# Attention's transposes as pairs of 64-row products into two banks, with a new order of the instructions

## The chip, the cores and the metric

The kernel runs on one core of one Trainium2 chip. The metric is the time of one execution in microseconds (us) on the device; a kernel is run several times and the median counts. Five engines work side by side, each through its own queue in order: TensorE (PE in the profile, its loading of stationary operands PEld), VectorE (DVE), ScalarE (ACT), GpSimd (POOL) and SyncE (SP, which here issues the DMAs).

## The reference

Four batches of eight heads go through an attention whose weak scores are cut off; its output goes through two feed-forward layers.

```python
scores = scale * np.matmul(q, k.transpose(0, 1, 3, 2))      # (4, 8, 576, 576), head size 64
thresh = np.max(scores, axis=-1, keepdims=True) - tau
scores = np.where(scores >= thresh, scores, -1000000000.0)
scores = scores - np.max(scores, axis=-1, keepdims=True)
attn = np.exp(scores)
attn = attn / (np.sum(attn, axis=-1, keepdims=True) + 1e-09)
out = np.matmul(attn, v)
...
g = h * np.tanh(sp)                 # h = x @ w_in (512 to 2048), sp = softplus(h); then g @ w_out
...
return (silu * val @ w_out)         # silu and val from x @ w_gate, x @ w_val (512 to 1536)
```

All numbers are float32.

## The kernel before

The first part of the program is the attention, the second the two layers (`moes`); the change is in the attention alone. The attention works on 16 pairs of heads. The queries of a pair are cut into chunks of 64 per head: chunks 0 to 3 of 128 rows of work per head, and a last one that holds both heads' last 64 queries, so that there are nine row blocks of 128 x 576 scores, numbered 0 to 8. In this text S, R, H, E, M, T, V, A and x are the kinds of step, with the number of the block behind them:

- S0, S2, S4, S6 (`scores`, line 97) make two blocks each with 64-row products, the two heads by turns, one on the upper and one on the lower 64 rows of the array; S8 makes one block with products over all 128 rows. A block takes two neighbouring banks of the eight in PSUM, so S0 to S6 take four.
- R (`rowmax`, L105, DVE) reads a block's maximum, H (`thresh`, L109, POOL) makes the threshold, E (`expo`, L115, ACT) the exponential, M (`mask`, L123, DVE) masks it and gives the block's two banks back.
- T (`trans`, L151 and L148, PE) transposes the masked weights of a pair of blocks, 128 x 128 at a time, nine such squares for chunks 0 to 3 and four and a rest for the last; V (`evac`, L157, L160, L164, ACT) copies the squares from PSUM into the tile `pt`. T takes one bank. Squares are taken in groups of three.
- A (`av`, L174, PE) multiplies `pt` with the values: A0 for the first four blocks (256 queries), A1 for the other five (320). Each is cut in two parts (`PARTS`). It takes one bank until x copies it out (x0 on ACT, L204; x1 on DVE, L202).
- At the end of a pair POOL adds a small number to the row sums (`added`, L178), DVE takes reciprocals (`recip`, L182, L183) and turns them (L187), and DMAs spread them over the rows.

What stands when on each engine is written out by a planner (`Plan`): each step has a rank from the table `RANK`, which differs for the first, second and last pair and is one row for the rest, and the planner places banks and steps by its own table of costs. Engines then work strictly in that order. Beside the attention the planner puts steps that prepare the first weights (L498 to L512, the names cn, cu, cl) and pieces of the layers' input (xo) on DVE, ACT and POOL.

Of the kernel before, what the change touches and what calls it, by code (L numbers as in the profile page):

```python
# [16 lines left out]
P = 128  # L17
# [19 lines left out]
def attention(tc, cst, q, k, v, x, beside, parked, S=576):  # L37
# [100 lines left out]
    def trans(p, c, m0, n):  # L138
        d = st[p]
        if m0 == 0 and c in (0, 2):  # L140
            d["pt", c // 2] = pw.tile([P, 9, 320], F32, tag="pt", name=f"pt{p}_{c // 2}", bufs=SLOTS["pt"])
        g = bank(p, "T", c, m0)
        d["g", c, m0] = g.rearrange("p (m c) -> p m c", m=4)
        for m in range(n):
            o = 128 * (m0 + m)
            if c == 4 and m0 == 4:
                if m == 0:
                    nc.tensor.transpose(g[0:64, 0:128], d["pp", c][:, o:o + 64], idf)  # L148
                    continue
                o -= 192  # L150
            nc.tensor.transpose(g[:, 128 * m:128 * m + 128], d["pp", c][:, o:o + 128], idf)  # L151

    def evac(p, c, m0, n):
        d = st[p]
        t, g = d["pt", min(c // 2, 1)], d["g", c, m0]
        if c < 4:
            nc.scalar.copy(out=t[:, m0:m0 + n, 128 * (c % 2):128 * (c % 2) + 128], in_=g[:, 0:n])  # L157
        elif m0 == 0:
            for h in range(2):
                nc.scalar.copy(out=t[:, 5 * h:5 * h + 4, 256:320], in_=g[:, :, 64 * h:64 * h + 64])  # L160
        else:
            for h in range(2):
                a = slice(64 * h, 64 * h + 64)
                nc.scalar.copy(out=t[a, 4, 256:320], in_=g[a, h, a])  # L164
# [71 lines left out]
    for p in range(NP):  # L236
# [14 lines left out]
        for i in range(9):  # L251
            c, h = divmod(i, 2)
            if not h:
                n = 2 if i < 8 else 1
                t = .77 if i < 8 else .81
# [5 lines left out]
            for m0, n in (((0, 3),), ((3, 3), (6, 3)))[h] if i < 8 else ((0, 4), (4, 2)):  # L261
                g = (p, "T", c, m0, 0)
                op("PE", (.109 * n, .109 * n + .164), trans, c, m0, n, key=("T", c, m0), after=[("M", i)] + [("T", 2 * min(c // 2, 1), 0)] * (m0 > 0 or c not in (0, 2)) + [("T", c, 3)] * (m0 == 6) + [("T", 4, 0)] * (c == 4 and m0 > 0), take=["b1"] + ["pt"] * (m0 == 0 and c in (0, 2)), free=["pp"] * (m0 == (6 if c < 4 else 4)))
                op("ACT", (.367, .485) if c < 4 else (.545, .658) if m0 == 0 else (.33, .44), evac, c, m0, n, key=("V", c, m0), after=[("T", c, m0)], free=[g])
            if i in (3, 8):
                u = int(i == 8)
                ready = [("V", y, z) for y in ((0, 1), (2, 3))[u] for z in (0, 3, 6)] + [("V", 4, 0), ("V", 4, 4), ("A", 0)] * u + [("v", "load")]
# [845 lines left out]
```

## Time and profile before

| | before |
|---|---|
| median of 3 runs | 1075.63 us (1073.8 to 1077.04) |
| the profiled execution's own time | 1075.19 us |
| its span, first to last instruction | 1073.4 us |
| PE busy | 1052.0 us, 98% of the span |
| DVE, ACT, POOL busy | 775.1, 649.0, 262.6 us |
| first scores, last product of the attention | 7.05 us, about 278 us |

The span is what the profile shows of an execution; 1.8 us of the execution's own time lie around it. Busy time of PE holds the time in which products wait on one another in the array, so that a busy PE need not be a PE at its limit. The profile's lines name engine, line of the program, operation and tiles (out<-in).

### The profile page before, as it was taken

What the parts mean: (1) busy time and instruction counts of PE and PEld (TensorE: products, weight loads), DVE (VectorE), ACT (ScalarE), POOL (GpSimd) and SP (SyncE); (2) the same over time, 40 slices, a digit from 0 to 9 for tenths busy, and PEclk for the clock granted to TensorE, in tenths of its full rate; (3) what the DMA queues carried; (4) which work ended last, traced back from release to release, by engine and by line L of the source; (5) the groups of instructions that cost most, each with busy time, mean ns of one, the idle gap of its engine ahead of it and who ended that gap; (6) DMA issues with size and microseconds to landing.
All of it is one profiled execution on the core that took longest, in us unless ns stands there. A gap on an engine that the chain in (4) does not pass through costs nothing.

```text
span 1073.4 us, 17930 instructions
## 1 busy us (share of the span) xinstructions
PE 1052.0 (98%) x6532; PEld 949.0 (88%) x6532; DVE 775.1 (72%) x1436; ACT 649.0 (60%) x1286; POOL 262.6 (24%) x401
## 2 busy tenths in 40 slices
PE   7999999999999999999999999999999999999998
PEld 6666676676899999999999999999999999999997
DVE  7888888888788465557377776974778686786645
ACT  6788888888877675455346555664445454444331
POOL 3467667676211120012011001110111011010000
PEclk9999999999999999999999999999999999999999
DMA  3234222243867876577567696688888788887793
GB/s 95 86 98 145 75 84 70 80 145 108 312 260 279 286 254 217 178 256 257 175 216 254 207 344 240 247 312 303 313 287 297 258 297 311 277 296 244 234 309 122
DMA packets 56775, 236.90 MB, mean 221 GB/s; under 512 B 8816, under 2 KB 9072, under 8 KB 56688
## 3 DMA queue, kind: packets, MB, share of 16 engines
q1 hardware_dynamic: 56688, 235.77, 63.5%
q8 instruction: 51, 0.84, 0.3%
q14 instruction: 36, 0.29, 0.1%
HBM read 197.92 MB, written 37.82 MB: 220 GB/s over the span
## 4 chain that ended last, share of the span: by engine, by line
PE 91%; ACT 3%; issue 1%; DVE 1%; DVEq 0%; ACTq 0%
PE ha L808 23%; PE y L934 18%; PE hb L808 17%; PE y L936 14%; PE banks L174 7%; PE banks L97 7%; PE banks L151 5%; ACT pt L157 1%; ACT e L115 1%; PE banks L148 0%; ACT g L841 0%; DVE g L844 0%; ACT c L853 0%; DVE sm L105 0%; ACT L853 0%
## 5 line engine op out<-in xcount | busy, mean ns | idle before, releaser
L512 POOL TENSOR_TENSOR cn<-cn,cl 128x512 int32<-128x512 int32 x68 | 93.4, 1374 | 631.3 <-DVE cn L509 449.1
L934 PE MATMUL y<-g,wo 128*128 128x384 f32 x1152 | 227.8, 334 | 1.6 <-DVE wo L535 0.9
L934 PEld LDWEIGHTS y<-g,wo 128*128 128x128 f32 x1152 | 202.1, 188 | 2.3 <-DVE wo L535 1.1
L952 DVE TENSOR_TENSOR acc<-y,acc 128x512 f32<-128x512 f32 (+2 forms) x163 | 100.0, 626 | 108.2 <-PE y L936 63.5
L936 PE MATMUL y<-wo,g 128*128 128x512 f32 (+1 forms) x654 | 166.6, 391 | 0.0
L808 PE MATMUL hb<-xp,wb 128*128 128x384 f32 x720 | 138.4, 334 | 0.0
L808 PE MATMUL ha<-xp,wb 128*128 128x384 f32 x720 | 138.3, 334 | 0.0
L936 PEld LDWEIGHTS y<-wo,g 128*128 128x128 f32 x654 | 120.5, 188 | 18.9
L123 DVE SCALAR_TENSOR_TENSOR pp<-banks,sm,e 128x576 f32<-128x576 f32 x144 | 114.9, 815 | 21.2 <-ACT e L115 15.1
L808 PEld LDWEIGHTS ha<-xp,wb 128*128 128x128 f32 x720 | 126.6, 188 | 3.1
L844 DVE TENSOR_TENSOR g<-c,g 128x384 fp32r<-128x384 f32 x168 | 103.1, 615 | 36.0 <-ACT g L841 35.3
L808 PEld LDWEIGHTS hb<-xp,wb 128*128 128x128 f32 x720 | 126.4, 188 | 1.5
L841 ACT CAST g<-c 128x384 fp32r<-128x384 f32 x168 | 86.2, 514 | 63.1 <-DVE c L877 31.0
L115 ACT ACTIVATE e<-banks,sm 128x576 f32<-128x576 f32 x144 | 106.5, 754 | 12.9 <-DVE sm L105 12.2
L105 DVE TENSOR_REDUCE sm<-banks 128x1 f32<-128x576 f32 x144 | 101.7, 751 | 13.4 <-PE banks L97 13.1
L853 ACT ACTIVATE c<-c 128x384 f32<-128x384 f32 x144 | 75.4, 525 | 52.0 <-DVE c L829 51.5
L157 ACT COPY pt<-banks 128x384 f32<-128x384 f32 x192 | 89.9, 490 | 24.4 <-PE banks L151 22.6
L151 PE MATMUL banks<-idf,pp 128*128 128x128 f32 x656 | 94.8, 280 | 3.6 <-DVE pp L123 3.1
L819 ACT COPY u<-ha 128x384 f32<-128x384 f32 x60 | 28.8, 480 | 112.9 <-PE ha L808 112.8
L151 PEld LDWEIGHTS banks<-idf,pp 128*128 128x128 f32 x656 | 71.1, 141 | 25.7 <-ACT pt L157 8.3
L174 PE MATMUL banks<-pt,vn 128*64 128x256 f32 (+1 forms) x640 | 88.4, 413 | 0.9 <-ACT pt L164 0.9
L808 PE MATMUL ha<-xp,wa 128*128 128x384 f32 x360 | 73.5, 340 | 0.8 <-ACT acc L204 0.8
(90 smaller groups left out, 1576.6 us busy)
## 6 DMA issues: line engine op xcount, KB each, us to landing
raw<-in_dram SPq DMA_DIRECT2D x68, 512.0 KB
xp<-x20T SPq DMA_DIRECT2D x24, 768.0 KB
xp<-x21T SPq DMA_DIRECT2D x20, 768.0 KB
xp<-x22T SPq DMA_DIRECT2D x20, 768.0 KB
xp<-x20B SPq DMA_DIRECT2D x18, 768.0 KB
xp<-x10T SPq DMA_DIRECT2D x15, 768.0 KB
xp<-x21B SPq DMA_DIRECT2D x15, 768.0 KB
xp<-x22B SPq DMA_DIRECT2D x15, 768.0 KB
```

Of the source, the lines that this page charges most:

```text
L105: nc.vector.tensor_reduce(out=d["nm"][:, i:i + 1], in_=d["s", i], op=ALU.max, axis=AX.X, negate=True)
L115: nc.scalar.activation(out=e, in_=d["s", i], func=AF.Exp, bias=d["nm"][:, i:i + 1])
L123: nc.vector.scalar_tensor_tensor(out=d["pp", c][:, 576 * h:576 * h + 576], in0=d["s", i], scalar=d["th"][:, i:i + 1], in1=d["e", i], op0=A ...
L151: nc.tensor.transpose(g[:, 128 * m:128 * m + 128], d["pp", c][:, o:o + 128], idf)
L157: nc.scalar.copy(out=t[:, m0:m0 + n, 128 * (c % 2):128 * (c % 2) + 128], in_=g[:, 0:n])
L174: nc.tensor.matmul(out=d["av", u][64 * h:64 * h + 64, 0:n], lhsT=d["vn"][:, 5 * h + j], rhs=d["pt", u][:, 5 * h + j if j < 4 else 4, 0:n], ...
L512: nc.gpsimd.tensor_tensor(out=self.n[key], in0=self.n[key], in1=self.l[key], op=ALU.add)
L808: nc.tensor.matmul(out=tiles[bank, q], lhsT=w[:, a, w0 + P * d:w0 + P * d + P], rhs=x[:, z, d], start=k in (1, 5, 2) and d == 0 and y == 0 ...
L844: (V if GLOW[L] == "DVE" else nc.gpsimd).tensor_tensor(out=tiles["g", j, s][:, 1], in0=tiles[nm, q], in1=f(tiles["g", j, s][:, 0]), op=ALU ...
L934: nc.tensor.matmul(out=y[:, 0:C], lhsT=w[:, a, P * d:P * d + P], rhs=h[:, x], **m)
L936: nc.tensor.matmul(out=y[:, c0:c1], lhsT=h[:, x, P * d:P * d + P], rhs=w[:, a, c0:c1], **m)
L952: V.tensor_tensor(out=a, in0=y, in1=a, op=ALU.add)
```

## The change

A square of 128 x 128 is no longer transposed by one product over 128 rows but by two over 64 rows, upper and lower by turns, into two neighbouring banks; the stationary operand is 64 rows of 128 columns, the moving one a 64 x 64 identity. Groups are four and five squares in place of three, three and three, so that a chunk has two V in place of three, of 512 and 640 elements a row in place of 384. T takes two banks in place of one. `pt` has ten columns of squares in place of nine. The planner's costs of the transposes (`TCOL`), of the copies and of the turns between kinds of products are new, and `RANK` with all of its numbers. The layers' code is the same.

```diff
-            d["pt", c // 2] = pw.tile([P, 9, 320], F32, tag="pt", name=f"pt{p}_{c // 2}", bufs=SLOTS["pt"])
-        g = bank(p, "T", c, m0)
-        d["g", c, m0] = g.rearrange("p (m c) -> p m c", m=4)
+            d["pt", c // 2] = pw.tile([P, 10, 320], F32, tag="pt", name=f"pt{p}_{c // 2}", bufs=SLOTS["pt"])
+        at = 512 * plan.got[p, "T", c, m0][0]
+        g = d["g", c, m0] = bk[:, at:at + 1024].rearrange("p (b m c) -> p b m c", b=2, m=8)
         for m in range(n):
-            o = 128 * (m0 + m)
-            if c == 4 and m0 == 4:
-                if m == 0:
-                    nc.tensor.transpose(g[0:64, 0:128], d["pp", c][:, o:o + 64], idf)
-                    continue
-                o -= 192
-            nc.tensor.transpose(g[:, 128 * m:128 * m + 128], d["pp", c][:, o:o + 128], idf)
+            for b in range(2):
+                rows, o = slice(64 * b, 64 * b + 64), 128 * (m0 + m)
+                if c == 4 and m0 == 4:
+                    a, e = 512 - 64 * b, 64 + 64 * b
+                    nc.tensor.transpose(g[0:e, b, 0], d["pp", c][rows, a:576], idf[rows, rows])
+                else:
+                    nc.tensor.transpose(g[:, b, m], d["pp", c][rows, o:o + 128], idf[rows, rows])
...
         if c < 4:
-            nc.scalar.copy(out=t[:, m0:m0 + n, 128 * (c % 2):128 * (c % 2) + 128], in_=g[:, 0:n])
+            nc.scalar.copy(out=t[:, m0:m0 + n, 128 * (c % 2):128 * (c % 2) + 128].rearrange("p m (b c) -> p b m c", b=2), in_=g[:, :, 0:n])
         elif m0 == 0:
-            for h in range(2):
-                nc.scalar.copy(out=t[:, 5 * h:5 * h + 4, 256:320], in_=g[:, :, 64 * h:64 * h + 64])
+            nc.scalar.copy(out=t[:, :, 256:320].rearrange("p (h m) c -> p h m c", h=2)[:, :, 0:4], in_=g[:, :, 0:4])
...
-            for m0, n in (((0, 3),), ((3, 3), (6, 3)))[h] if i < 8 else ((0, 4), (4, 2)):
+            for m0, n in (((0, 4),), ((4, 5),))[h] if i < 8 else ((0, 4), (4, 1)):
...
-    TURN = dict(ST=.106, SA=.175, TS=.08, TA=.09, AS=.15, AT=.15)
+    TURN = dict(ST=.02, SA=.15, TS=.02, TA=.1, AS=.15, AT=.15)
...
+TCOL = .065
```

The new ranks move steps at three places that matter below. The first is PE in the middle of the attention, from S0 of a pair to its S2 (pp_2 and pp_4 hold the weights of the pair before, the L97 rows with kh and qh are scores). Before:

```order
L151 MATMUL banks<-idf,pp_2_973 128x128 [waits DVE_49]
L151 MATMUL banks<-idf,pp_2_973 128x128 x2
L151 MATMUL banks<-idf,pp_4_1048 128x128 x4
L151 MATMUL banks<-idf,pp_3_1031 128x128 [waits Activation_49]
L151 MATMUL banks<-idf,pp_3_1031 128x128 x5
L151 MATMUL banks<-idf,pp_3_1031 128x128 [waits Activation_49]
L151 MATMUL banks<-idf,pp_3_1031 128x128 x2
L97 MATMUL banks<-kh_943,qh_997 128x320 [waits Activation_49]
L97 MATMUL banks<-kh_943,qh_997 128x320 [waits DVE_49]
```

And now:

```order
L151 MATMUL banks<-idf,pp_3_1162 128x64 [waits DVE_49]
L151 MATMUL banks<-idf,pp_3_1162 128x64 x7
L151 MATMUL banks<-idf,pp_4_1183 128x64 [waits Activation_49]
L151 MATMUL banks<-idf,pp_4_1183 128x64 x7
L151 MATMUL banks<-idf,pp_3_1162 128x64 [waits Activation_49]
L151 MATMUL banks<-idf,pp_3_1162 128x64 x9
L97 MATMUL banks<-kh_1053,qh_1034 128x320 [waits Activation_49]
L97 MATMUL banks<-kh_1053,qh_1034 128x320 [waits DVE_49]
```

Sixteen squares stood there, and now thirteen, as 26 products; the scores behind them wait as before for ACT (their first half's bank) and DVE (their second half's).

The second place is DVE, from a pair's last M to the next pair's first M (sm_1768 and sm_2003 belong to the old pair, sm_1993 and sm_2265 to the new one). Before:

```order
L123 SCALAR_TENSOR_TENSOR pp_4_1968,sm_1768<-banks,sm_1768,e_8_1958 128x576
L105 TENSOR_REDUCE sm_1993<-banks 128x1 x2
L123 SCALAR_TENSOR_TENSOR pp_0_2015,sm_1993<-banks,sm_1993,e_0_2004 128x576
L182 RECIPROCAL rr_156<-sm_1768 128x4x2
L183 RECIPROCAL rr_156<-sm_1768 128x1
```

And now:

```order
L123 SCALAR_TENSOR_TENSOR pp_4_2237,sm_2003<-banks,sm_2003,e_8_2219 128x576
L181 RECIPROCAL rr_156<-sm_2003 128x4x2
L182 RECIPROCAL rr_156<-sm_2003 128x1
L105 TENSOR_REDUCE sm_2265<-banks 128x1
L186 STREAM_TRANSPOSE rr_156<-rr_156 128x32
L105 TENSOR_REDUCE sm_2265<-banks 128x1
L123 SCALAR_TENSOR_TENSOR pp_0_2297,sm_2265<-banks,sm_2265,e_0_2278 128x576
```

The two reciprocals, which read what POOL has added to the sums, have moved from behind the new pair's M0 to ahead of its R0. A pair's x1 has moved too, on the same engine, from behind M4 of the next pair to ahead of it: the row `L201 COPY acc<-banks 128x320` now stands between R5 and M4. On POOL the sum that the reciprocals read has an xo step just ahead of it in five of the 16 pairs, in two of these two of them.

The third place is ACT between E1 and E3 of a pair (L164, now L163, are the two small copies of the last chunk of the pair before; pt_0 is the new pair's tile). Before:

```order
L164 COPY pt_1_1703<-banks 64x64 [waits PE_49]
L164 COPY pt_1_1703<-banks 64x64
L115 ACTIVATE e_2_1833<-banks,sm_1768 128x576 [waits DVE_49,Activation_49]
```

And now:

```order
L163 COPY pt_1_2182<-banks 64x64 [waits PE_49] x2
L157 COPY pt_0_2321<-banks 128x2x4x64 [waits DVE_49,PE_49]
L115 ACTIVATE e_2_2343<-banks,sm_2265 128x576 [waits DVE_49,Activation_49]
L115 ACTIVATE e_3_2346<-banks,sm_2265 128x576 [waits DVE_49,Activation_49]
```

The new pair's first V (V0) now stands ahead of E2, where it stood behind it.

## Rows read from the trace of the kernel before

**Rows 1.** Stages: us, busy time of each engine (instructions), TensorE's granted clock, DMA share, GB/s.

```profile
62.00:261.90 199.90, 193.14 (x1637) 138.04 (x1637) 173.09 (x384) 170.77 (x364) 142.00 (x260) 1.00 0.31 97
```

**Rows 2.** Timeline of PE, one pair: start, us, operation, count, [idle before, releaser].

```profile
155.89 0.41 PE L97 MATMUL banks<-kh,qh 64*128 64x320 f32 x2
...
156.67 0.28 PE L97 MATMUL banks<-kl,qh 64*128 64x256 f32 x2
156.88 1.97 PE L151 MATMUL banks<-idf,pp 128*128 128x128 f32 x16
159.39 0.73 PE L97 MATMUL banks<-kh,qh 64*128 64x320 f32 x2 [0.54 <-ACT pt L157]
159.71 0.56 PE L97 MATMUL banks<-kh,ql 64*128 64x320 f32 x2
...
165.66 1.30 PE L174 MATMUL banks<-pt,vn 128*64 128x320 f32 x8
...
167.36 0.41 PE L97 MATMUL banks<-kh,qh 64*128 64x320 f32 x2
```

**Rows 3.** Timeline of DVE over the same pair.

```profile
156.99 1.42 DVE L105 TENSOR_REDUCE sm<-banks 128x1 f32<-128x576 f32 x2 [0.20 <-PE banks L97]
...
158.83 0.82 DVE L123 SCALAR_TENSOR_TENSOR pp<-banks,sm,e 128x576 f32<-128x576 f32 x1
...
160.82 1.42 DVE L105 TENSOR_REDUCE sm<-banks 128x1 f32<-128x576 f32 x2
162.51 0.82 DVE L123 SCALAR_TENSOR_TENSOR pp<-banks,sm,e 128x576 f32<-128x576 f32 x1 [0.28 <-ACT e L115]
...
164.63 1.42 DVE L105 TENSOR_REDUCE sm<-banks 128x1 f32<-128x576 f32 x2 [0.28 <-PE banks L97]
166.33 0.82 DVE L123 SCALAR_TENSOR_TENSOR pp<-banks,sm,e 128x576 f32<-128x576 f32 x1 [0.28 <-ACT e L115]
...
167.07 0.55 DVE L202 COPY acc<-banks 128x128 f32<-128x128 f32 x2
...
168.46 2.08 DVE L105 TENSOR_REDUCE sm<-banks 128x1 f32<-128x576 f32 x3
...
171.93 0.81 DVE L123 SCALAR_TENSOR_TENSOR pp<-banks,sm,e 128x576 f32<-128x576 f32 x1
...
173.56 0.76 DVE L105 TENSOR_REDUCE sm<-banks 128x1 f32<-128x576 f32 x1 [0.20 <-PE banks L97]
```

**Rows 4.** Timeline of ACT over the same pair.

```profile
161.14 0.42 ACT L164 COPY pt<-banks 64x64 f32<-64x64 f32 x2 [0.24 <-PE banks L151]
161.67 0.74 ACT L115 ACTIVATE e<-banks,sm 128x576 f32<-128x576 f32 x1
```

**Rows 5.** Timeline of PE, first pair, scores that follow scores.

```profile
8.76 0.31 PE L97 MATMUL banks<-kh,qh 64*128 64x320 f32 x2
...
9.44 0.28 PE L97 MATMUL banks<-kl,qh 64*128 64x256 f32 x2
```

**Rows 6.** Groups by line and shape, 0 to 440 us: busy us, mean ns | idle before.

```profile
L157 ACT COPY pt<-banks 128x384 f32<-128x384 f32 x192 | 89.9, 490 | 24.4 <-PE banks L151 22.6
...
L151 PEld LDWEIGHTS banks<-idf,pp 128*128 128x128 f32 x656 | 71.1, 141 | 25.7 <-ACT pt L157 8.3 <-DVE pp L123 6.2 <-ACT e L115 5.4
...
L160 ACT COPY pt<-banks 128x256 f32<-128x256 f32 x32 | 10.7, 405 | 0.0
...
L626 POOL TENSOR_TENSOR xo<-acc,xo 128x384 fp32r<-128x384 f32 x12 | 12.0, 1009 | 1.4 <-ACT xo L625 1.3
...
L148 PEld LDWEIGHTS banks<-idf,pp 128*64 128x64 f32 x16 | 1.7, 108 | 2.2 <-ACT pt L160 1.8
```

**Rows 7.** Timeline of all engines, last pair's last M, sum and reciprocal.

```profile
271.63 0.81 DVE L123 SCALAR_TENSOR_TENSOR pp<-banks,sm,e 128x576 f32<-128x576 f32 x1
...
272.54 0.26 POOL L178 TENSOR_SCALAR sm<-sm 128x9 f32<-128x9 f32 x1 [1.70 <-DVE pp L123]
...
272.84 0.20 DVE L182 RECIPROCAL rr<-sm 128x8 f32<-128x8 f32 x1 [0.38 <-POOL sm L178]
```

More of the change, by code (lines that the diff above doesn't have):

```diff
@@ L163, in evac @@
                 a = slice(64 * h, 64 * h + 64)
-                nc.scalar.copy(out=t[a, 4, 256:320], in_=g[a, h, a])
+                nc.scalar.copy(out=t[a, 4, 256:320], in_=g[a, h, 0])
     def av(p, u, j0, j1):
@@ L254, in attention @@
                 n = 2 if i < 8 else 1
-                t = .77 if i < 8 else .81
+                t = .77 if i < 8 else .95
                 op("PE", (t, t + .21), scores, i, key=("S", i), after=[("q", "lo"), ("k", "lo")] + [("t",), ("S", 6)] * (i == 8), take=[f"b{2 * n}"], free=["k", "qt", "q"] if i == 8 else [])
@@ L260, in attention @@
             op("DVE", (.738, .815), mask, i, key=("M", i), after=[("E", i), ("H", i)] + [("M", i - 1)] * (i > 0), take=["pp"] if h == 0 else [], free=[(p, "S", i - h, h), "e"])
-            for m0, n in (((0, 3),), ((3, 3), (6, 3)))[h] if i < 8 else ((0, 4), (4, 2)):
+            for m0, n in (((0, 4),), ((4, 5),))[h] if i < 8 else ((0, 4), (4, 1)):
                 g = (p, "T", c, m0, 0)
-                op("PE", (.109 * n, .109 * n + .164), trans, c, m0, n, key=("T", c, m0), after=[("M", i)] + [("T", 2 * min(c // 2, 1), 0)] * (m0 > 0 or c not in (0, 2)) + [("T", c, 3)] * (m0 == 6) + [("T", 4, 0)] * (c == 4 and m0 > 0), take=["b1"] + ["pt"] * (m0 == 0 and c in (0, 2)), free=["pp"] * (m0 == (6 if c < 4 else 4)))
-                op("ACT", (.367, .485) if c < 4 else (.545, .658) if m0 == 0 else (.33, .44), evac, c, m0, n, key=("V", c, m0), after=[("T", c, m0)], free=[g])
+                op("PE", (TCOL * n, TCOL * n + .164), trans, c, m0, n, key=("T", c, m0), after=[("M", i)] + [("T", 2 * min(c // 2, 1), 0)] * (m0 > 0 or c not in (0, 2)) + [("T", 4, 0)] * (c == 4 and m0 > 0), take=["b2"] + ["pt"] * (m0 == 0 and c in (0, 2)), free=["pp"] * (m0 == 4))
+                t = .094 + .091 * n if c < 4 or m0 == 0 else .33
+                op("ACT", (t, t + .118), evac, c, m0, n, key=("V", c, m0), after=[("T", c, m0)], free=[g])
             if i in (3, 8):
                 u = int(i == 8)
-                ready = [("V", y, z) for y in ((0, 1), (2, 3))[u] for z in (0, 3, 6)] + [("V", 4, 0), ("V", 4, 4), ("A", 0)] * u + [("v", "load")]
+                ready = [("V", y, z) for y in ((0, 1), (2, 3))[u] for z in (0, 4)] + [("V", 4, 0), ("V", 4, 4), ("A", 0)] * u + [("v", "load")]
                 for n, (j0, j1) in enumerate(PARTS):
@@ L415, in order @@
             for *x, z in o["drop"]:
-                at, w = self.got[tuple(x)][z], 2 if x[1] == "S" else 1
+                at, w = self.got[tuple(x)][z], 1 if x[1] == "A" else 2
                 self.bank[at:at + w] = [done + self.SEM[e]["PE"]] * w
```

4 lines of the change are left out of this document (2 added, 2 removed).

## The prediction

> **What bounds the kernel now.** The stages come first. In the steady part of the attention, from 62 to 261.9 us, PE is busy 193.1 of 199.9 us at the full granted clock (1.00, the 2.4 GHz level), DVE 173.1, ACT 170.8, POOL 142 [rows 1]. One pair of heads takes 16.57 us there (R0 at 156.99, the next pair's R0 at 173.56 [rows 3]), so that the stretch holds 12.06 pairs, and a pair costs PE 16.0, DVE 14.35 and ACT 14.2 us. By these sums PE is the bound and the other two have some 2 us to spare. The layers behind the attention are untouched; what the change is worth is what it takes from the 16.57, about 15 times (16 pairs, of which one fills and drains).
>
> Then the timelines of one pair, to see which wait ends last. PE waits once, 0.54 us ahead of S2 [rows 2]. But DVE waits too, and its waits form a second loop nearly as long as PE's: rowmax, exponential, mask, and only then two banks for the next scores. Eight banks hold the four of one S and little more; the second half of S2 started at 159.71, when M0 (from 158.83) had just ended [rows 2, 3], and so it is in every S. From R to R this loop now reads [rows 3]: R0 to M0 1.84, M0 to R2 1.99, R2 to M2 1.69, M2 to R4 2.12, R4 to M4 1.70, M4 to R6 2.13, R6 to M8 3.47, M8 to the next R0 1.63; sum 16.57. So I do not price the change by what it takes from PE alone: PE's loop may shorten below DVE's, and then DVE's decides.
>
> **The change: PE's part.** A pair has 42 squares. Sixteen of them take 1.97 us from the first's start to the last's end [rows 2], about 0.109 us each. What a square costs as two products over 64 rows no row shows. The moving operand halves, from 128 columns to 64: by that 0.055, if the two halves run side by side as the two heads' scores do: from the first to the last of their six pairs of products 0.68 us pass [rows 5], the time of 1472 moving columns (three times 320, twice 256) and not of twice as many. The stationary load takes 141 ns for 128 columns and 108 for 64 [rows 6], so that 64 columns more cost 33, and 128 some 0.066 without the fixed part. The other end is a pair of score products with 256 columns, which also loads 128 columns twice: 256 of the 1472 columns in 0.68 us, 0.118. I take 0.066, since the transposes' own loads are the nearest rows: 42 squares then cost 2.8 in place of 4.6 us, 1.8 less. Scores and transposes now use the array in one shape: S takes 0.68 us from its first to its last product where it follows scores [rows 5] and 0.78 where it follows a transpose [rows 2]; with the like at the other ends some 1 us of PE goes. PE's work falls to about 13.2 us a pair, and it stops being the bound.
>
> A rule of the Trainium skill speaks against the price of a square. "TensorE: Matmul & The Clock Gate", section on LDWEIGHTS, says that a stationary load takes the time of its columns, at 1.2 GHz, however few its rows. By it each half-square would load as long as the whole one did, an estimate of 107 ns; the two side by side would give a square no gain, the case of the first rival. The rows here (33 ns for 64 columns) speak for a load half as long; no row has a transpose's load over 64 rows.
>
> **The loop of DVE, step by step, after the change** (R0 at 0; hops as the rows have them):
> - R0 to M0: 0.85 to E0 (R2 160.82, E2 161.67 [rows 3, 4]) and 0.84 to M0 (161.67 to 162.51). 1.70. The 0.14 more of before belongs to a step of weights in between.
> - M to the next R, three times: 0.88 until the second half of S may start (158.83 to 159.71 [rows 2, 3]), then 1.10 from S to R (155.89 to 156.99), less the 0.10 that S no longer loses at its start or loses while it waits. 1.88 each, before 1.99, 2.12 and 2.13: a gain of 0.60.
> - R2 to M2: R2 is at 3.58. V0 now stands ahead of E2. The rest of the last chunk is transposed when S2 is through (3.36), the two small copies end near 4.28 (0.42 [rows 4]), and V0 follows: 384 elements take 490 ns and 256 take 405 [rows 6], so 512 some 575, of which about 0.1 lies beside the next; 0.47. E2 starts at 4.75 in place of 4.43, M2 at 5.59: 2.01, before 1.69. A loss of 0.32.
> - R4 to M4: x1 now stands ahead of M4. S4 is through at 7.25, five squares and a turn to 7.67, the second part of A1 1.30 and 0.05 more [rows 2], so x1 runs from 9.02 for 0.55 [rows 3], in pairs with one piece a little less. M4 at 9.52 in place of 9.17: 2.05, before 1.70. A loss of 0.35.
> - R6 to M8: the same steps on DVE, 3.47.
> - M8 to the next R0: the reciprocals now stand ahead of R0 and wait for POOL's sum. In the last pair, where nothing hid it, M8 at 271.63, the sum at 272.54, the reciprocal at 272.84 [rows 7]: 1.21, and 0.23 for the two reciprocals until R0, since the first two overlap. 1.44, before 1.63, where PE and a step of weights held R0.
>
> Sum 16.31, against 16.57: 0.26 us a pair, 15 times 3.9 us. PE's own way from S6 to the next R0 (167.36 to 173.56, 6.20 now [rows 2, 3]) loses 0.2 on seven squares and some turns, to about 5.8; DVE's is 1.00 and 3.47 and 1.44, 5.9; they end almost together, so that PE gives no more back there.
>
> The bounds of the square: at 0.055 the part ahead of x1 gains 0.05 a pair, 0.8 us in all; at 0.118 it loses 0.2 there and 0.1 ahead of V0, and the gain falls to nothing. The thirteen squares between S0 and S2 cost nothing either way: S2 waits for M0 and not for them. The ten columns of `pt`, the fewer V (two in place of three: by the same rows 1.05 us in place of 1.10 a chunk) and the DMAs, which are as before, are covered: ACT has 2 us of idle a pair, and where V stands in the way it is in the list.
>
> The sum is made against the profiled execution, 1075.19 us; its median is 0.44 higher. 1075.2 less 3.9 is 1071.3, and **1071.5 us** stands for both. About 0.3%, 3.2 us, is what a measurement of this kernel can tell from no change, so the forecast itself lies at the edge of that.
>
> **The rivals.**
> - *The squares are not cheaper* (the change doesn't do what it says): a square stays at 0.109 or 0.118, because loads, not moving columns, set it. Then the loop is 16.6 and PE's work 15.1: no change, 1075 to 1077. For it: the score pairs at 0.118; against it: the loads' slope. If the halves ran one behind the other, 0.2 a square, PE would be the bound again near 18 us, and the kernel 20 us slower; the scores' halves running together excludes that all but for a few in a hundred.
> - *The new waits don't bite*: V0 and x1 are done before they are in the way, since PE, with 3 us to spare, comes to T and A earlier than I laid out. Then both hops are 1.70, the loop is 15.65, and 15 times 0.92 is 14 us: 1061. For it: PE is no more the bound, and each engine's work is under 14.4. Against it: both T stand behind an S that itself waits for M, so that PE's spare time lies ahead of S and not behind it.
> - *POOL's sum holds DVE* (slower): the reciprocals stand ahead of R0, and an xo step of 1.0 us [rows 6] stands just ahead of the sum on POOL in five of the 16 pairs, in two of them twice. If POOL reaches it only when M8 ends, R0 and the whole loop wait 1 us more for each, 7 in all: 7 less 3.9 is 3 us slower, 1078 to 1079. It decides from the point where POOL's lateness adds up to over 3.9 us. Against it: POOL is idle 29% of the stretch [rows 1], and by the order it should come to xo some 1.0 us before M8 ends.
>
> **How the numbers follow.** Forecast 0.40 (own range 1068 to 1075), the waits that don't bite 0.34, squares not cheaper 0.12, slower by POOL's sum or the like 0.14. Faster by over 0.3%: 0.58 of the forecast's 0.40 and nearly all of 0.34, 0.56. Slower: 0.14 and a little of the other cases, 0.16. Same: 0.28. The range reaches from the case of waits that don't bite, with a microsecond for the square at 0.055, to the slower case: 1059 to 1080; under 2 in 10 lie outside.
>
> **What the profile of the changed kernel would show.** A transposing pair's step near 0.066 us, and S behind T at 0.68. PE idle over 2 us a pair, most of it ahead of S2, S4 and S6, ended by DVE's M or ACT's V. On DVE: x1 directly ahead of M4 with a wait for PE, a wait for POOL ahead of the reciprocals, hops of 2.0 from R2 to M2 and from R4 to M4. The period near 16.3 us and the layers of the same length. The prediction is wrong if the period is under 16 with idle time on DVE spread elsewhere, if a square costs over 0.1, or if the granted clock falls under 1.00 in the attention now that PE waits more.

## The result: 1% slower, and the profile after

The changed kernel took 1085.55 us (median of 3 runs, 1084.98 to 1088.07) where the kernel before took 1075.63: 1.010 times as long, with an interval of 1.0065 to 1.0134. The forecast of 1071.5 was wrong in its sign, and the time lies outside the range. Run again later, it took 1087.51 us (1.0121, 1.0105 to 1.0137).

The page of the changed kernel, its span, the busy time of each engine, TensorE's granted clock in 40 slices, and the group of the transposes' loads (busy us, mean ns):

```profile
span 1083.7 us, 19221 instructions
...
PE 1045.4 (96%) x7172; PEld 940.8 (87%) x7172; DVE 776.4 (72%) x1436; ACT 647.5 (60%) x1206; POOL 262.8 (24%) x401
...
PEclk8899899989999999999999999999999999999999
...
L151 PEld LDWEIGHTS banks<-idf,pp 64*128 64x128 f32 x1280 | 55.9, 144 | 35.8 <-ACT pt L157 16.5
```

The layers are as long as before (their first product starts at 289.2 us in place of 278.8, and the span is longer by the same 10.3): all of the loss is in the attention. The first ten slices are the attention, and four of their clock digits are an 8: the granted clock falls there, again and again, to its 1.2 GHz level. (A figure such as 0.90 is the mean over a stretch, part of it at 1.2 and the rest at 2.4 GHz; in this text a half-clock stretch is such a part.) The kernel before had 1.00 there [rows 1]. The same stretch as [rows 1], and then some pairs, each from its R0 to the next R0 (columns as in [rows 1], the granted clock third from the end; the pair from 147.41 is a plain one, with no step of weights on DVE):

```profile
62.00:261.90 199.90, 180.22 (x2062) 125.50 (x2060) 170.54 (x374) 167.61 (x300) 140.44 (x256) 0.95 0.34 104
...
24.29:43.86 19.57, 16.55 (x180) 11.69 (x178) 13.86 (x30) 13.71 (x24) 6.97 (x17) 0.83 0.16 47
113.12:130.27 17.15, 15.39 (x172) 10.84 (x170) 14.67 (x34) 14.49 (x26) 12.28 (x24) 0.90 0.25 74
130.27:147.41 17.14, 15.71 (x180) 11.27 (x180) 13.97 (x34) 14.74 (x27) 12.55 (x23) 0.90 0.26 76
147.41:163.72 16.31, 14.84 (x180) 10.39 (x180) 13.88 (x33) 14.00 (x25) 12.81 (x23) 1.00 0.27 78
...
214.21:231.78 17.57, 16.11 (x180) 10.74 (x180) 14.91 (x35) 14.11 (x25) 11.25 (x22) 0.90 0.38 119
231.78:249.09 17.31, 15.90 (x180) 10.86 (x180) 13.89 (x34) 13.38 (x24) 12.60 (x23) 0.90 0.29 100
```

A plain pair at full clock takes 16.31 us, what the prediction's list of hops came to. But few pairs are plain. Where the granted clock is 0.90 or 0.91 they take 17.1 to 18.0, and the second pair, at 0.83, takes 19.57 (16.38 in the kernel before).

What PE did before the clock fell, on the pair from 130.27 (timeline of PE; the clock is at its lower level from 133.0 on, and the products get longer there):

```profile
130.12 0.71 PE L151 MATMUL banks<-idf,pp 64*128 64x64 f32 x16
131.27 0.53 PE L151 MATMUL banks<-idf,pp 64*128 64x64 f32 x10 [0.43 <-ACT pt L157]
132.39 0.99 PE L97 MATMUL banks<-kh,qh 64*128 64x320 f32 x2 [0.59 <-ACT pt L159]
...
133.18 0.72 PE L97 MATMUL banks<-kl,qh 64*128 64x320 f32 x2
```

Thirteen squares of short products, and among and behind them waits of 0.43 and 0.59 us for copies on ACT. In the kernel before sixteen longer squares took 1.97 us at this place, with one wait of 0.54 [rows 2].

DVE's timeline over the plain pair from 147.41, the rows that answer to [rows 3]:

```profile
147.41 0.74 DVE L105 TENSOR_REDUCE sm<-banks 128x1 f32<-128x576 f32 x1
...
149.09 0.82 DVE L123 SCALAR_TENSOR_TENSOR pp<-banks,sm,e 128x576 f32<-128x576 f32 x1 [0.19 <-ACT e L115]
...
150.96 1.42 DVE L105 TENSOR_REDUCE sm<-banks 128x1 f32<-128x576 f32 x2
152.93 0.82 DVE L123 SCALAR_TENSOR_TENSOR pp<-banks,sm,e 128x576 f32<-128x576 f32 x1 [0.55 <-ACT e L115]
...
154.80 1.42 DVE L105 TENSOR_REDUCE sm<-banks 128x1 f32<-128x576 f32 x2 [0.30 <-PE banks L97]
156.45 0.49 DVE L201 COPY acc<-banks 128x320 f32<-128x320 f32 x1 [0.23 <-PE banks L173]
156.86 0.81 DVE L123 SCALAR_TENSOR_TENSOR pp<-banks,sm,e 128x576 f32<-128x576 f32 x1
...
158.88 2.09 DVE L105 TENSOR_REDUCE sm<-banks 128x1 f32<-128x576 f32 x3 [0.46 <-PE banks L97]
...
162.36 0.81 DVE L123 SCALAR_TENSOR_TENSOR pp<-banks,sm,e 128x576 f32<-128x576 f32 x1
...
163.57 0.21 DVE L181 RECIPROCAL rr<-sm 128x8 f32<-128x8 f32 x1 [0.40 <-POOL sm L177]
```

| hop | predicted | measured |
|---|---|---|
| R0 to M0 | 1.70 | 1.68 |
| M0 to R2, M2 to R4, M4 to R6 | 1.88 each | 1.87, 1.87, 2.02 |
| R2 to M2 (V0 ahead of E2) | 2.01 | 1.97 |
| R4 to M4 (x1 ahead of M4) | 2.05 | 2.06 |
| R6 to M8 | 3.47 | 3.48 |
| M8 to the next R0 | 1.44 | 1.36 |
| sum | 16.31 | 16.31 |

The hops agree within 0.14, and their differences cancel: that the sums agree to the hundredth is luck.

### The profile page after: what moved, and what is told of

The parts are those of the page before. It is cut to its first block, busy times and chain, and to the rows that moved or that the text cites. A ratio compares the mean times of both kernels' runs of the same rounds, so it can differ in the third digit from the quotient of the medians.

```text
span 1083.7 us, 19221 instructions
## 1 busy us (share of the span) xinstructions
PE 1045.4 (96%) x7172; PEld 940.8 (87%) x7172; DVE 776.4 (72%) x1436; ACT 647.5 (60%) x1206; POOL 262.8 (24%) x401
## 4 chain that ended last, share of the span: by engine, by line
PE 86%; ACT 6%; DVE 5%; issue 3%; POOL 0%; DVEq 0%; ACTq 0%; POOLq 0%
PE ha L809 23%; PE y L935 18%; PE hb L809 17%; PE y L937 14%; PE banks L97 6%; PE banks L173 5%; ACT e L115 3%; PE banks L151 2%; ACT pt L157 2%; DVE pp L123 2%; DVE sm L105 2%; PE banks L67 1%; DVE cn L507 0%; ACT pt L159 0%; DVE g L845 0%
## 5 line engine op out<-in xcount | busy, mean ns | idle before, releaser
L123 DVE SCALAR_TENSOR_TENSOR pp<-banks,sm,e 128x576 f32<-128x576 f32 x144 | 112.4, 813 | 17.1 <-ACT e L115 14.8
L115 ACT ACTIVATE e<-banks,sm 128x576 f32<-128x576 f32 x144 | 101.9, 746 | 6.3 <-DVE sm L105 6.1
L157 ACT COPY pt<-banks 128x640 f32<-128x640 f32 (+1 forms) x128 | 80.7, 644 | 34.5 <-PE banks L151 31.2
L173 PE MATMUL banks<-pt,vn 128*64 128x256 f32 (+1 forms) x640 | 98.6, 449 | 1.9 <-DVE pp L123 0.9
L151 PEld LDWEIGHTS banks<-idf,pp 64*128 64x128 f32 x1280 | 55.9, 144 | 35.8 <-ACT pt L157 16.5
L151 PE MATMUL banks<-idf,pp 64*128 64x64 f32 x1280 | 70.4, 235 | 14.8 <-ACT pt L157 7.3
L173 PEld LDWEIGHTS banks<-pt,vn 128*64 128x64 f32 x640 | 45.3, 148 | 34.4 <-issue 8.7
```

The costliest lines, as they stand in the source:

```text
L115: nc.scalar.activation(out=e, in_=d["s", i], func=AF.Exp, bias=d["nm"][:, i:i + 1])
L123: nc.vector.scalar_tensor_tensor(out=d["pp", c][:, 576 * h:576 * h + 576], in0=d["s", i], scalar=d["th"][:, i:i + 1], in1=d["e", i], op0=A ...
L151: nc.tensor.transpose(g[:, b, m], d["pp", c][rows, o:o + 128], idf[rows, rows])
L173: nc.tensor.matmul(out=d["av", u][64 * h:64 * h + 64, 0:n], lhsT=d["vn"][:, 5 * h + j], rhs=d["pt", u][:, 5 * h + j if j < 4 else 4, 0:n], ...
```

## The experiments

Three theories were tried. Theory 1: the granted clock falls because PE now waits more with short products, and that is the loss. Theory 2: the new order is slow by itself. Theory 3, formed after the first four runs: DVE's steps of weights (cn) lengthen the loop now that DVE bounds the pair. Each ratio is to runs of the kernel before on the same chip (medians 1074.3 to 1075.5 us); times from different chips differ by up to a microsecond for that alone.

**Products in PE's waits, and elsewhere.** Five products a pair that write zeros to columns nobody reads (`wz` is a tile of zeros): two behind the four squares of the last chunk, three behind the five squares ahead of S2. `FILL` gives their number:

```diff
+        for w in range(FILL(p, c, m0)):
+            nc.tensor.matmul(out=g[:, w % 2, 5:8], lhsT=wz[:, 0:P], rhs=wz[:, 0:192], start=True, stop=True)
```

> The changed kernel, with five more products a pair on PE, which write zeros to columns that nothing reads: two behind the four squares of the last chunk, three behind the five squares ahead of S2, where PE waits for ACT (0.43 and 0.59 us in the changed kernel). Theory 1, the clock: the changed kernel is slow because the granted clock falls to the 1.2 GHz level after PE has waited there. Then the seven half-clock stretches between 62 and 273 us vanish, every pair takes the 16.3 to 16.6 us that the pairs at full clock take now, and the time comes down by the 7.3 us that pairs of 17.1 to 18.0 us lose now: 1077 to 1079 us, with the two long half-clock stretches before 40 us still there. Theory 2, the order: the new order and the loop of DVE cost the 10 us by themselves and the clock is a by-product. Then the time stays at 1084 to 1088 us.

Measured: 1088.72 us, 1.0126 (1.0111 to 1.0141). Four half-clock stretches between 62 and 290 us in place of seven. Plain pairs stayed at 16.3, so that the products cost nothing there, but pairs with steps of weights were as long as before or longer: the fourth, seventh and eleventh, in which the clock still fell, took 19.08, 17.89 and 19.16. Theory 1 had named 1077 to 1079: as the whole of the loss it fell here.

With four more behind each group in the first two pairs, and sixteen behind the second scores of the first:

> As the kernel with five more products a pair, and more of the same in the first two pairs: sixteen behind the second scores of the first pair, where PE waits 2.1 us for the first mask, and four behind each group of transposes until the middle of the second pair. Theory 1, the clock: no half-clock stretch before 290 us, the first three pairs take about what they took before (48 us in place of 53), the others 16.3 to 16.5, and the time is what the sum of the prediction said without a fall of the clock, 1070 to 1074 us. Theory 2, the order: 1082 to 1088 us.

Measured: 1094.98 us, 1.0201 (1.0163 to 1.0239). From 88 us on the clock held, and yet the pairs there were 16.29, 16.69, 16.78, 16.31, 16.33, 16.37, 17.74, 16.40, 16.90, 16.31, 17.73. The long ones, but for the last, were those with a DVE step of weights. The head became slower, 42.1 us for the first two pairs in place of 35.4: the readers of these banks wait for the added products (before 70 us ACT's copies wait 12.4 us in all for them), a cost of the experiment and not of the change.

The same five products behind two other groups, the four squares of chunk 2 (two) and the five of chunk 1 (three):

> The same five products a pair, but behind two other groups of transposes, those between S4 and S8, where PE hardly waits (0.19 us). Theory 1, the clock: the wait ahead of S2 is as it was, the half-clock stretches stay, and the products add up to 0.3 us a pair where they stand in the way: 1085 to 1090 us. Should any added product do, wherever it stands, the time falls as with the products ahead of S2, to 1077 to 1079 us. Theory 2, the order: 1085 to 1090 us as well.

Measured: 1092.74 us, 1.0165 (1.015 to 1.018). Plain pairs became 16.7 to 16.9, so PE has no room there. Of the clock something else was expected than came: the stretches were to stay, and between 62 and 290 us there were two in place of seven, with a full clock from the fifth pair to the fifteenth. So the added products hold the clock here too, away from the wait ahead of S2; that this wait by itself brings the falls is not shown.

**The order with whole squares.** The changed order, groups and banks, each square one product over 128 rows:

```diff
-            for b in range(2):
-                rows, o = slice(64 * b, 64 * b + 64), 128 * (m0 + m)
...
-                    nc.tensor.transpose(g[:, b, m], d["pp", c][rows, o:o + 128], idf[rows, rows])
+            nc.tensor.transpose(g[:, m], d["pp", c][:, o:o + 128], idf)
```

> The changed kernel's order, groups of four and five and pairs of banks, but each transpose a product over 128 rows again, as before. Theory 1, the clock: PE has more to do (0.109 us a square in place of 0.063) and waits less, the clock stays at 1.00, and the loop is that of the first rival of the prediction, 16.5 to 16.7 us a pair: 1074 to 1078 us. Theory 2, the order: the time stays at 1083 to 1088 us although the clock is full.

Measured: 1096.51 us, 1.0204 (1.0189 to 1.0219). Stages of this kernel, one plain pair:

```profile
153.21:170.86 17.65, 16.68 (x137) 11.63 (x138) 13.99 (x32) 13.83 (x25) 13.31 (x23) 1.00 0.25 72
```

The clock is full and the pair takes 17.65 us. The shorter squares are thus worth 1.34 us a pair in the new order (17.65 to 16.31), and the new order costs 1.08 with the old squares (16.57 to 17.65): the net gain of 0.26 is the difference of two numbers over 1 us. Here theory 2 is right, of whole squares; theory 1 had expected 16.5 to 16.7 us a pair.

**The same kernel again.** No edit; the clock falls at other times in each execution.

> The changed kernel again. If the clock sets the spread of its runs, the time falls as the mean granted clock rises, by 0.5 to 0.8 us for each 0.001, as in the runs of the kernels with added products; 1083 to 1089 us at 0.976 to 0.983. If not, times and clocks go apart.

Measured: 1087.51 us, and the runs 1086.35 at a mean clock of 0.978, 1086.9 at 0.979, 1088.12 at 0.977, 1091.08 at 0.974: time and clock go together, by about 1 us for each 0.001, more than expected. Its pairs, as above:

```profile
24.41:42.34 17.93, 14.94 (x180) 11.05 (x178) 13.86 (x30) 13.70 (x24) 6.99 (x17) 0.90 0.16 50
...
131.04:147.35 16.31, 14.84 (x180) 10.41 (x180) 13.88 (x34) 14.63 (x27) 12.50 (x23) 1.00 0.26 80
147.35:164.50 17.15, 15.72 (x180) 11.11 (x180) 13.96 (x34) 13.98 (x25) 12.80 (x23) 0.90 0.25 74
...
218.78:235.64 16.86, 14.87 (x180) 10.44 (x180) 14.90 (x36) 14.10 (x25) 11.21 (x22) 1.00 0.39 124
235.64:251.95 16.31, 14.84 (x180) 10.41 (x180) 13.88 (x33) 13.36 (x24) 12.54 (x23) 1.00 0.31 106
```

This is the clock's price, measured without any edit. The eighth pair takes 17.14 us at 0.90 in one execution and 16.31 at 1.00 in the other; the ninth 16.31 at 1.00 and 17.15 at 0.90; the thirteenth 17.57 and 16.86; the fourteenth 17.31 and 16.31; the second 19.57 at 0.83 and 17.93 at 0.90. Of all pairs whose clock differs between the two executions, most were 0.5 to 1.2 us longer in the one with a stretch more, and the second, third, eleventh and last 1.4 to 1.9.

**Steps of weights cut to 8 columns.** In the attention DVE's two steps of weights work on 8 columns in place of 512, in the kernel before, the changed one, and the changed one with products in its waits; the second step likewise, and POOL's step behind them no longer reads what they write:

```diff
-            V.tensor_scalar(out=self.n[key], in0=self.raw[key][:, :, 1], scalar1=-0x80000000, scalar2=None, op0=ALU.bitwise_and)
+            V.tensor_scalar(out=self.n[key][:, 0:8], in0=self.raw[key][:, 0:8, 1], scalar1=-0x80000000, scalar2=None, op0=ALU.bitwise_and)
```

> The kernel before, with DVE's two steps of weights (cn) in the attention cut from 512 columns to 8, in the same places of the order; the weights made there are wrong, which leaves work out and changes no other time. Theory 3, steps of weights in the loop: in the kernel before PE bounds the pair and DVE has 2 us to spare, so that these steps cost nothing there. The pairs stay at 16.57 us, only the three that are longer (18.20, 16.79, 16.85) may lose some of it: 1073 to 1075 us, 0 to 2 us less. Rival: the steps cost their own time wherever they stand; then 4 to 6 us less, 1069 to 1071.

Measured: 1074.52 us, 0.9998 (0.9989 to 1.0008). No gain, and pairs of 16.57.

> The changed kernel with the same steps of weights cut to 8 columns (the weights made there are wrong). Theory 3: in the changed kernel DVE's own loop bounds the pair, so that each step of weights lengthens its pair; with full clock pairs without one took 16.29 to 16.40 us, pairs with one or two 16.69, 16.78, 16.90 and 17.74. Cut, they give back 0.4, 0.5, 0.6, 1.4 and, in the two pairs before 80 us, 2 to 3 us: 1079 to 1082 us in place of 1085.5, with half-clock stretches still there. Rival, the clock alone: the long pairs are long because of the clock; then 1084 to 1087.

Measured: 1083.33 us, 1.009 (1.0068 to 1.0111), about 2 us less than the changed kernel by the medians and 1.1 by the ratios, which is not clear of their intervals; the expected 1079 to 1082 was missed. In its profile the fourth pair came from 18.00 to 16.96, the sixth from 16.70 to 16.30, the eleventh from 17.74 to 17.51 only.

The products alone, sixteen behind the second scores of the first pair and the rest in waits:

> The changed kernel with products that write zeros only where PE waits: sixteen behind the second scores, six, six, two and three in the waits of the first two pairs, and seven ahead of S2 in every pair. Theory 1, the clock, as far as it still stands: no or one half-clock stretch before 290 us, the first four pairs take 66 to 69 us in place of 71.3 (64.7 before), the pairs from the fifth on 183.8 in place of 186.5 (182.9 before): 1078 to 1082 us. Rival: the products themselves delay the loop as much as the clock did: 1085 to 1089.

Measured: 1089.36 us, 1.0136 (1.0103 to 1.017). Its four runs are 1084.22 at a clock of 0.996, 1088.78 at 0.990, 1089.94 at 0.989 and 1093.46 at 0.984: 0.8 us for each 0.001. The median is the rival's; the first four pairs took 72.5 in place of 66 to 69, but those from the fourth to the fourteenth, all at full clock, 183.8 in place of 187.3. Three of them:

```profile
113.99:130.79 16.80, 15.48 (x179) 10.97 (x176) 14.66 (x34) 14.48 (x26) 12.24 (x24) 1.00 0.26 75
...
179.81:197.54 17.73, 15.93 (x187) 11.40 (x189) 16.22 (x36) 14.71 (x26) 13.31 (x24) 1.00 0.34 117
...
213.94:230.83 16.89, 15.93 (x187) 11.40 (x187) 14.91 (x36) 14.11 (x25) 11.22 (x22) 1.00 0.37 124
```

The eleventh pair is 17.73 us with a full clock and 17.74 in the changed kernel at 0.90: there the clock is not what is long, DVE is (16.22 us busy in place of 13.9).

> Both edits of the changed kernel together: products in PE's waits, and DVE's steps of weights cut to 8 columns (the weights made there are wrong). If clock and steps of weights are two separate causes, their gains add: every pair from the fourth to the fourteenth at 16.3 to 16.5 us, and 1073 to 1077 us, at most 2 us from the kernel before with the same cut. If one of them was only a sign of the other, the time is that of the better single edit, within 1 us.

Measured: 1084.53 us, 1.0085 (1.0057 to 1.0112), 4.8 us less than with products alone; its runs are 1080.17 and 1080.55 at 0.998, 1084.53 and 1084.85 at 0.992, 1088.53 at 0.987. By the medians the two gains did not add: this is 1.2 us over the better single edit. In the profiles they did, from the fourth pair to the fourteenth: 187.3 us in the changed kernel, 185.9 with short steps, 183.8 with products, 181.6 with both; but the first two pairs, with the added products and a clock of 0.67 in the first, took 38.7 in place of 35.4. And the eleventh pair was still 17.05. A timeline of this kernel shows why (DVE and POOL):

```profile
187.84 1.42 POOL L231 TENSOR_TENSOR ql<-qn,qh 128x576 fp32r<-128x576 f32 x1
...
188.01 1.28 DVE L527 TENSOR_SCALAR cn<-raw 128x8 int32<-128x8 int32 x1
```

A step of 8 columns took 1.28 us: it ended at 189.29, POOL's step beside it at 189.26. Such a step takes 0.16 us elsewhere in this kernel. It waits for POOL, and cutting its columns doesn't take that away, so these runs undercount.

**Products that hold nobody.** Four of 256 columns behind the last chunk's four squares, nine in the first two pairs:

> The changed kernel with products that write zeros only where neither PE nor a reader of their banks is waited for: four of 256 columns behind the four squares of the last chunk (their copy comes 0.9 us later, and PE waits 0.43 there), and nine in the first two pairs. Theory 1, the clock: where the granted clock of a run is 0.995 or more, this kernel shows what the new order is worth without the clock: the head as before or 1 us longer, plain pairs 16.3, pairs with steps of weights on DVE 16.7 to 17.7: 1075 to 1079 us; runs at a lower clock lie higher, by about 0.7 us for each 0.001 of it. Rival, the head's order is slow by itself: 1081 us or more at a clock of 0.995.

Measured: 1086.08 us, 1.0102 (1.0086 to 1.0117), at clocks of 0.987 to 0.990; the head kept its half-clock stretches, and no run reached the 0.995 of the expectation, which so was not tested.

**Two hops undone.** On that kernel, x1 behind M5, V0 behind E2, and both (ranks `x`, `x1` and `V` alone):

> The same, with the copy x1 behind M5 on DVE in place of ahead of M4. By the prediction's hops, x1 ahead of M4 makes the way from R4 to M4 2.05 to 2.13 us in place of 1.70; behind M5 it falls into the 0.40 us that DVE waits for S6. Then plain pairs take 15.9 to 16.0 us and the time is 3 to 5 us under the kernel it is taken from. Rival: A1 ends as late as before and holds S6 and T on PE, and the pair stays at 16.3.

> The same as the first, with the copy V0 behind E2 on ACT in place of ahead of it. By the prediction's hops, V0 makes the way from R2 to M2 1.97 us in place of 1.69; behind E2 the pair is 0.28 us shorter, 16.0 to 16.1, and the time 3 us under the kernel that it is taken from. Rival: V0, later by 0.7 us, holds the transposes behind it, and the loss comes back at S4: 16.3.

> Both moves. If the two hops are separate terms of DVE's loop, as the prediction's sum has them, plain pairs take 15.6 to 15.7 us, and the time is 6 to 8 us under the kernel that it is taken from: 1067 to 1072 us at a full clock, under the kernel before. If another engine's loop is close behind (PE's 14.9 us of work, ACT's 14.0), the second move brings less than the first.

Measured: 1098.1 us (1.0214, 1.0179 to 1.0249), 1081.86 (1.0063, 1.0048 to 1.0078) and 1095.92 (1.0195, 1.018 to 1.0211). With x1 late, plain pairs took 16.9 to 17.4 us: PE's second group T of a chunk had to wait for M4 (timeline of PE),

```profile
217.16 0.53 PE L153 MATMUL banks<-idf,pp 64*128 64x64 f32 x10 [0.73 <-DVE pp L125]
```

and S6 stands behind it. With V0 late plain pairs stayed at 16.3 (timeline of DVE):

```profile
150.03 1.42 DVE L107 TENSOR_REDUCE sm<-banks 128x1 f32<-128x576 f32 x2
151.72 0.82 DVE L125 SCALAR_TENSOR_TENSOR pp<-banks,sm,e 128x576 f32<-128x576 f32 x1 [0.27 <-ACT e L117]
...
153.59 1.42 DVE L107 TENSOR_REDUCE sm<-banks 128x1 f32<-128x576 f32 x2
155.52 0.49 DVE L205 COPY acc<-banks 128x320 f32<-128x320 f32 x1 [0.52 <-PE banks L177]
155.93 0.81 DVE L125 SCALAR_TENSOR_TENSOR pp<-banks,sm,e 128x576 f32<-128x576 f32 x1
```

R2 to M2 did come down to 1.69, but x1 then waited 0.52 us for A1, and R4 to M4 went up to 2.34. The list of hops is a true record of the loop and a false table of prices: what is taken out of one hop comes back in the next. That kernel was 4 us faster all the same: the steps of weights came to stand elsewhere (its fourth pair 16.31 in place of 17.65), and the clock held in the eleventh pair (17.64 in place of 19.23).

**The clock held in the head.** In the first two pairs the products stand in the bank whose rowmax comes last:

```diff
+        for _ in range({(0, 2): 16, (1, 2): 6}.get((p, i), 0)):
+            n = 512 * plan.got[p, "S", i][1]
+            nc.tensor.matmul(out=bk[:, n:n + 192], lhsT=wz[:, 0:P], rhs=wz[:, 0:192], start=True, stop=True)
```

> As the kernel with products that hold nobody, and in the first two pairs sixteen and six products of 192 columns more behind the scores of the second chunk, in the bank whose rowmax comes latest. If the head is slow because of the clock: no half-clock stretch before 40 us, the first pair 14.0 to 14.6 us and the second 16.4 to 17.0 (13.5 and 16.4 before; 15.8 and 19.6 in the changed kernel), and 1076 to 1080 us at a clock of 0.996 or more. If the order is slow there by itself: first and second pair 15.5 or more and 17.8 or more at full clock, and 1081 us or more.

> The same with V0 behind E2, in which the steps of weights came to stand where they cost less (pairs three to ten took 3 us less together). If the clock is the head's cost: 1073 to 1077 us at a clock of 0.996, about the time of the kernel before. Otherwise 1079 or more.

Measured: 1082.91 us, 1.0072 (1.006 to 1.0084), and with V0 behind E2 1077.97, 1.003 (1.0019 to 1.0041; 1076.67 at a clock of 0.998). In the first of the two, pairs one and two took 15.65 and 17.39, with one half-clock stretch left there, in pair one. The second pair, at full clock, thus lies between the two expectations (16.4 to 17.0 if the clock is the head's cost, 17.8 or more if the order is), and the time is over the 1080 of the first. The second kernel is a microsecond over its 1073 to 1077. In the first kernel's profile the clock still fell in the third, seventh and eleventh pairs, which have steps of weights, and in the last, but not in the fourth, whose steps are as long as the eleventh's. DVE and PE in the eleventh:

```profile
186.27 1.63 DVE L522 TENSOR_SCALAR cn<-raw 128x512 int32<-128x512 int32 x1
...
189.16 0.54 DVE L208 COPY acc<-banks 128x128 f32<-128x128 f32 x2
...
189.75 0.52 PE L156 MATMUL banks<-idf,pp 64*128 64x64 f32 x9 [1.03 <-DVE acc L208]
...
190.59 0.42 PE L99 MATMUL banks<-kh,qh 64*128 64x320 f32 x2 [0.32 <-ACT pt L164]
```

DVE's step delays x1, x1 holds the bank that T needs, PE waits 1.03 and 0.32 us, and at 191.2 the clock falls: the pair took 19.12. With the same steps and no fall it was 17.73 above.

**No steps of weights on DVE.** Both steps left out in the attention:

> The changed kernel with the products of the last kernel that held the clock in the head, and without DVE's two steps of weights in the attention (left out altogether; the weights made there are wrong). If these steps lengthen the loop, with the time that they wait for POOL: the pairs that took 16.66 to 19.1 us with such steps come to 16.3 to 16.5 at full clock, and the whole lies 4 to 6 us under the kernel with them, 1077 to 1079 us at a clock of 0.993 to 0.995. If other steps of weights, on ACT and POOL, make these pairs long, less than 1.5 us.

> The same with V0 behind E2. Pairs that took 17.36, 17.62 and 16.70 us come to 16.3 to 16.4; 2 to 4 us under the kernel with the steps, 1074 to 1076 us at 0.996 to 0.998, about the kernel before. Should it come to 1072 or less, the change would be worth something once clock and steps of weights are out of the way.

> The kernel before without these steps (the weights made there are wrong). DVE has 2 us to spare in each pair there, and they cost nothing: 1073.5 to 1075.5 us, pairs of 16.57 as before. If they cost their time in the kernel before too: 1070 to 1072.

Measured: 1075.72 us, 1.0011 (1.0002 to 1.002); 1074.35, 1.0001 (0.9992 to 1.001); and the kernel before without them 1074.78, 0.9999 (0.999 to 1.0008). In the changed order with V0 ahead of E2 the steps cost 7.2 us (1082.91 to 1075.72; 6.6 by the ratios, since the chips differ), with V0 behind E2, where they stand elsewhere, 3.6 (3.1 by the ratios); 4 to 6 and 2 to 4 were expected. In the kernel before they cost nothing clear of the noise (its third pair took 17.23 in place of 18.20 and its first, with a half-clock stretch, 14.08 in place of 13.53). Pairs of the first of the three:

```profile
24.30:41.59 17.29, 15.32 (x192) 11.36 (x189) 14.04 (x32) 13.80 (x24) 6.89 (x16) 1.00 0.17 53
...
108.01:124.32 16.31, 15.43 (x184) 10.94 (x184) 13.87 (x33) 14.38 (x26) 11.93 (x24) 1.00 0.26 79
173.29:189.67 16.38, 15.51 (x182) 11.01 (x184) 13.99 (x34) 14.57 (x26) 12.66 (x24) 1.00 0.36 126
239.31:257.31 18.00, 16.93 (x208) 12.25 (x210) 14.18 (x34) 15.56 (x28) 10.73 (x23) 1.00 0.18 55
```

The eleventh pair has come from 19.12 to 16.38, and with the steps the clock's falls behind them are gone too: its rows show the lower level at 17.9 us, and then not before 301. One pair is long for another reason: the thirteenth, with a step of 1.04 us, took 16.88, and without it still 16.89. There an xo step on ACT stands ahead of V0, and M2 waits 1.05 us for E2 in place of the 0.55 of the plain pair (timelines of ACT and DVE):

```profile
210.28 0.51 ACT L646 CAST xo<-acc 128x384 fp32r<-128x384 f32 x1
...
212.14 0.82 DVE L129 SCALAR_TENSOR_TENSOR pp<-banks,sm,e 128x576 f32<-128x576 f32 x1 [1.05 <-ACT e L121]
```

## Why the prediction was wrong

From R0 to the next R0, in us (timelines of DVE in the profiled runs). The third column is the kernel with products in PE's waits, the last the one with products in the head and no steps of weights on DVE; both ran at a mean clock of 0.996.

| pairs | before | changed | products in the waits | products, no such steps |
|---|---|---|---|---|
| 1 and 2 | 29.91 | 35.35 | 34.26 | 33.11 |
| 3 | 18.20 | 17.91 | 20.56 | 17.49 |
| 4 to 14, sum | 182.9 | 187.3 | 183.8 | 180.2 |
| 15 | 16.58 | 17.18 | 17.84 | 18.00 |
| 16, to the first product of the layers | 22.29 | 22.92 | 24.31 | 21.58 |

The changed kernel loses 5.4 us in the first two pairs, 4.4 in the fourth to the fourteenth and 1.2 in the last two; the third is 0.3 shorter and the first R0 0.4 earlier. That makes the 10.3.

- **The loop of a plain pair** was right, hop by hop within 0.14. Over the fourth to the fourteenth pair, at full clock and without steps of weights, the gain is 2.7 us (182.9 to 180.2), where eleven times 0.26 make 2.9. PE's part was less right: the prediction had 13.2 us of work and over 2 us of waits a pair, and the plain pair has PE busy for 14.84 and idle for 1.47, of which 1.02 are the two waits for ACT shown above.
- **The square** was right in its size, 0.066 us: in the rows of PE above eight squares take 0.71 us and five 0.53, so three take 0.18, 0.06 each. The reason given for it, a load half as long, was not: a load over 64 rows took 144 ns, one over 128 rows 141 [rows 6]. "TensorE: Matmul & The Clock Gate", section on LDWEIGHTS in the Trainium skill, says that rows don't shorten a load. The trace agrees (with 144 ns in place of the estimate of 107), but two such loads and their products go by in 0.06 us a square, so they overlap one another, and the case of no gain for a square did not come.
- **The step that failed: "15 times".** The sum took the plain pair's gain for all pairs, 3.9 us, and put at nothing what else changes in them. From the fourth to the fourteenth pair the gain of 2.7 is outweighed by 3.6 us for DVE's steps of weights (183.8 to 180.2, both at full clock) and 3.5 for falls of the granted clock (187.3 to 183.8); the first two and the last two pairs lose 6.7 where one pair was left out as no change. In the kernel before, PE bounds the pair, DVE has 2 us to spare and its steps of weights vanish in them (0.9999 without them). The prediction saw one of them, took its 0.14 us out of R0 to M0 as "a step of weights in between", and left all of them out of the new loop. With DVE as the bound they cost their own time, the time that they wait for POOL, and in many executions a fall of the clock behind them. How much depends on where they stand, too: 7.2 us in one order and 3.6 in the other.
- **The granted clock.** The prediction named a fall under 1.00 as what would make it wrong and gave it neither a price nor a chance. Between two executions of the same program a stretch more cost 0.5 to 1.9 us.
- **First, second and last pairs.** "16 pairs, of which one fills and drains" was taken as no change, and the first two pairs hold the largest part of the loss, with no step of weights on DVE in them. With the clock nearly held they take 2.2 us less than in the changed kernel, but still 3.2 more than before; one half-clock stretch is left in the first, and one of that kind in the first pair of the kernel before without steps of weights cost 0.55 (14.08 for 13.53). The rest is the new order with the added products in it; the two were not separated, so that the cause stays open there. The fifteenth pair takes 0.6 more at full clock without added products (17.18) and 1.4 with them; why was not tried.
- **The rivals.** POOL's sum did not hold DVE: the reciprocal waited 0.40 us for it in the plain pair (0.38 in [rows 7]), and 0.48 and 0.49 in the two pairs with two xo steps ahead of the sum, where the rival had 2 us. "The new waits don't bite" was false: they are in the loop as laid out (1.97 and 2.06 us), though neither could be had back by a move of its own. That the squares are not cheaper would have cost far more than the 1075 to 1077 given: with whole squares a pair takes 17.65 us, 1.0 over the 16.6 worked out. PE is busy for 16.68 of them, so that PE probably bounds that order again; this was not tested.

No version of the change beat the kernel before; the nearest that computes the same, with the clock held and V0 behind E2, is 0.2 to 0.4% over it.

## What to carry to other kernels

When a change moves the bound from one engine to another, list everything that the new bounding engine does in the stretch, the side work too, and price it again: what was hidden under the old bound stands in the loop of the new one, for its whole time and for what it waits for. A gain per pass holds for the passes that look like the one it was read from; count those first, and price the first and the last passes by themselves. And when the engine that becomes idle is TensorE, give the fall of its granted clock a price from a row at the lower level and a chance, since the time that PE is spared can be taken back by running slower.

## What the runs showed of the hardware

DVE's two steps of weights (both on integers, from SBUF to SBUF, one with one input and one with two) and a POOL step beside them wait for each other to end. In the kernel before (timelines of DVE and of POOL):

```profile
156.10 0.69 DVE L509 SCALAR_TENSOR_TENSOR cn<-cu,cn 128x512 int32<-128x512 int32 x1
...
158.33 0.42 DVE L506 TENSOR_SCALAR cn<-raw 128x512 int32<-128x512 int32 x1
...
156.28 0.64 POOL L178 TENSOR_SCALAR sm<-sm 128x9 f32<-128x9 f32 x1 [0.43 <-DVE pp L123]
```

There POOL's sum, 0.26 us when alone [rows 7], took 0.64 and ended 0.13 after DVE's step. In the changed kernel most of DVE's steps came second, beside a longer step of POOL, and those took 0.96 to 1.68 in place of 0.42 and 0.69; in the kernel before only the third pair's did, 1.57 (timelines of DVE and of POOL):

```profile
187.44 1.64 DVE L507 TENSOR_SCALAR cn<-raw 128x512 int32<-128x512 int32 x1
...
187.38 1.42 POOL L222 TENSOR_TENSOR ql<-qn,qh 128x576 fp32r<-128x576 f32 x1
```

"SBUF — State Buffer" in the Trainium skill, section "SBUF: two separate sides", says that the two engines share one pair of ports, which for certain kinds of steps the first takes for its whole instruction while the other stands still. The 8-column step that took 1.28 us and ended 0.03 after POOL's step agrees.

In the pair shown from 130.12 the granted clock fell although no wait of PE was over 0.6 us; and it fell at other times in each execution of the same program, so that one program's times spread by up to 9 us with its mean clock (1084.22 at 0.996 to 1093.46 at 0.984).
